# Decoding the first layer's weights one or two units earlier, with a clamp and a low part moved to GpSimd

## The chip, the cores and the metric

The kernel runs on one core of a Trainium2 chip. Its time is the device time of one execution in microseconds, and lower is better. TensorE (PE) does the matrix products, VectorE (DVE), ScalarE (ACT) and GpSimd (POOL) the elementwise work, and SyncE (SP) issues the transfers from and to HBM.

## What is computed

An attention over columns, followed by two feed-forward layers without biases. N is 6016 tokens, C is 256, the hidden width is 2048:

```python
qn = q / (norm(q, axis=1) + 1e-06)          # q, k, v: 6016 x 256
kn = k / (norm(k, axis=1) + 1e-06)
s = kn.T @ qn / tau                          # 256 x 256
a = exp(s - s.max(-1)); a /= a.sum(-1) + 1e-09
x = v @ a                                    # 6016 x 256
h = x @ w_in;  x = (h * cos(h)) @ w_out      # first layer
h = x @ w_in2; out = (h * sigmoid(h)) @ w_out2   # second layer
```

The weights lie in HBM as 64-bit floating-point numbers, and the kernel turns them into 32-bit ones itself.

## The kernel before

**Stages.** The scores are summed over the tokens while q and k arrive. Softmax follows at about 49 us. From there the first layer runs over blocks of 512 tokens, and later the second layer beside it. The stretch of this case is the first 135 us. v @ a is never formed: `a` is multiplied into w_in, in four pieces called folds (`fold`, L705, tile `pw`), and block after block of v is multiplied with the folded weights (`wa`).

**Units.** The loop over `units` (L1143 on) handles one block of 512 tokens and one pair of 128-column parts of the hidden width in each turn. The first 16 turns alternate between blocks 0 and 1 in pairs of turns, so that unit 0 and 1 are of block 0, unit 2 and 3 of block 1, unit 4 and 5 of block 0 again with the next fold's weights. In turn i the program issues: the 12 matmuls of the first product (`emit_h`, L792, tile `h`); the matmuls of one fold in turns 3, 6 and 10; the split of the last unit's result into a high and a low part (`emit_split`, ACT `hi` L798, DVE `lo` L799); the cosine (ACT L1138, tile `t`) and the product with it (DVE L1140); some steps of decoding; then the 12 matmuls of the second product of the unit two turns back (`emit_o1`, L812, tile `o`). Turns 0, 2, 4, 8 and 12 need a small bound first (`bound_piece`, matmuls L439, DVE L446 and L447, tile `bound` or `o` with `smalls`), from which the cosine's scale comes; it needs the largest entry of the new fold (DVE L457) and the range of each 128 tokens (`firsts`, DVE L427). Products `h` and folds `pw` use two rooms of PSUM in turn, so that a fold has to wait until the product of the unit before the last has left its room.

**Decoding.** Each matrix of the first layer comes in four pieces of 1024 numbers for each of 128 partitions: W1 (tile `w`, raw `raw_w`), one for each fold, and WO1 (tile `wv_wo`, raw `raw_wo`, result `wo`). A piece takes these steps, each a call with a name of two letters, the second of them W or O for the matrix:

- l: the load, a transfer on SP's queue (L279).
- b, begin: ACT takes the magnitude of the upper word (L345), POOL rounds the lower word (L299).
- c, clamp: DVE limits the magnitude (L304) and shifts it (L312).
- j, join: DVE puts the sign in (L318), POOL adds the lower word (L321).
- s, split (WO1 alone): ACT writes the high part (L364), POOL the low part (L365).

Fold k needs the join of W1's piece k. The other names in the tables below are: x0 and x1, the range of v's block 0 and 1 (`span_of_first`, L427); lv, the load of block 1 (L410, tile `vraw`, which has one buffer); s1 and v1, its high part on ACT (L486) and its low part on DVE (`low`, L489, tile `xlo`); v0, the low part of block 0 on POOL; rs, the inverse sums of softmax (L685, L686); f, e, l and w with a number, the matmuls of a fold, its high part (ACT L714), its low part (DVE L736) and its largest entries (L457).

**What sets the order.** Every engine works through its instructions in the order in which the program issues them. The order of the steps is written by hand, in the string `BEFORE` for what comes ahead of the first unit and in the table `EARLY` for the turns: 'amid' ahead of the split, 'mid' between cosine and product, 'outer' behind the product. An engine that waits holds back all that stands behind it.

Of the kernel before, what the change touches and what calls it, by code (L numbers as in the profile page):

```python
# [9 lines left out]
F32 = mybir.dt.float32  # L10
# [5 lines left out]
AF = mybir.ActivationFunctionType  # L16
ALU = mybir.AluOpType
# [5 lines left out]
CH = C // P  # L23
# [7 lines left out]
BLOCKS = [(sum(SIZES[:i]), n) for i, n in enumerate(SIZES)]  # L31
# [27 lines left out]
THEN = ['', '', 'jO s0', '']  # L59
SIDE = [7, 11, 15, 20]  # L60
JOINED = 22
BEFORE = 'v0 sO T0 T1 bW rs f00 x0 lv l00 f01 w00 l01 w01 tb x1 s1 l'
TURNS = 16
FORMING = {
    12: 'A0', 13: 'A1', 15: 'B0', 16: 'B1', 17: 'V', 18: 'V', 19: 'V A2', 20: 'A3', 21: 'B2', 22: 'B3'
}
DOUBLED = (17, 22)
EARLY = {
    'amid': {3: 'f1', 6: 'f2', 10: 'f3'},
    'mid': {0: 'v1'},  # L70
    'outer': {
# [3 lines left out]
    },  # L75
}
assert sum(GROUPS) == NCK
# [3 lines left out]
PASSES = ((0, 0), (1, 0), (0, 1))  # L81
# [146 lines left out]
def direct(ctx, tc, qk, vT, tau, w_in1, w_out1, w_in2, w_out2, outT, dp, kept, within):  # L228
    nc = tc.nc
# [35 lines left out]
    class Weights:  # L265
# [123 lines left out]
    def columns(t):  # L389
        return t.rearrange("p (h b) -> p b h", h=2)  # L390
# [127 lines left out]
    rs = pp.tile([P, CH], F32, name="rs")  # L518
    W1 = w_in(w_in1, "w1", to=w1, pool=pp, bufs=4, size=LARGE)
# [3 lines left out]
        parts=[[t[:, i].rearrange("p m (f e) -> p (m f) e", e=C) for i in range(2)] for t in wo1],  # L523
# [5 lines left out]
    raw_v, low_v = {}, {}  # L529
# [3 lines left out]
        "v0": lambda: low_v.pop(0)(nc.gpsimd),  # L533
        "x0": lambda: span_of_first(0, raw_v.pop(0)),
        "lv": lambda: raw_v.update({1: load_v(1)}),
        "x1": lambda: span_of_first(1, raw_v[1]),
        "s1": lambda: low_v.update({1: split_v(1, raw_v.pop(1))}),
        "v1": lambda: low_v.pop(1)(),
        "l": WO1.load,
        "lW": W1.load,  # L540
        "bW": W1.begin,
        "aW": lambda: W1.begin(low="act"),
        "cW": W1.clamp,
        "jW": W1.join,
        "bO": WO1.begin,
        "aO": lambda: WO1.begin(low="act"),
# [5 lines left out]
    def steps_of(names):  # L552
        for name in names.split():
            calls[name]()
# [201 lines left out]
    T = [sc.tile([P, NS, HB], F32, name=f"t{k}") for k in range(2)]  # L756
    HI, LO = [[sc.tile([P, NU, HB], F32R, name=f"{s}{k}") for k in range(2)] for s in ("hi", "lo")]
# [7 lines left out]
    def flat(t):  # L765
        return plain_part(t).rearrange("p (s n) -> p s n", s=2)
# [17 lines left out]
    def emit_h(u):  # L784
        b, m = u
        n = BLOCKS[b][1]
        x = xparts[1, b]
        hp = ready.pop() if ready else h_tile(f"h{b}_{m}")
        for s in range(2):
            todo = [(wa_at(i, a, 2 * m + s), columns(x[k][:, a, :n])) for i, k in PASSES for a in range(CH)]  # L790
            for i, (lhsT, rhs) in enumerate(todo):
                nc.tensor.matmul(hp[:, s, :n], lhsT, rhs, start=(i == 0), stop=(i == len(todo) - 1))  # L792
        return hp

    def emit_split(i, u):
        n = BLOCKS[u[0]][1]
        t, hi, lo = [flat(x[i % 2]) for x in (T, HI, LO)]
        nc.scalar.activation(hi[:, :, :n], t[:, :, :n], AF.Copy)  # L798
        nc.vector.tensor_tensor(out=lo[:, :, :n], in0=t[:, :, :n], in1=hi[:, :, :n].bitcast(F32), op=ALU.subtract)  # L799
        return hi, lo  # L800

    def o1_room(b):
        if (1, b) not in state:
# [330 lines left out]
    def cosine_in(i, h):  # L1134
        b, m = units[i]
        out = flat(T[i % 2])
        j = m // 2 * FIRST + b
        nc.scalar.activation(out, h, AF.Sin, bias=half_pi, scale=smalls[:, j : j + 1] if b < FIRST else small[b])  # L1138
        steps_of(EARLY["mid"].get(i, ""))
        nc.vector.tensor_tensor(out=out, in0=h, in1=out, op=ALU.mult)  # L1140

    units = [(i // 2 % 2, i // 4 * 2 + i % 2) for i in range(TURNS)] + [(FIRST, m) for m in range(NPAIR)]
    LAG = 2  # L1143
    parts = {}
    pend = None
    vs = []
    for i, u in enumerate(units):
        b, m = u
        if i == TURNS - 1:
            pro.close()  # L1150
            rp = ctx.enter_context(tc.tile_pool(name="rp", bufs=1))
            wf = [rp.tile([P, 2, 2, 4, P], F32R, name=f"wf{k}") for k in range(4)]
            Y = rp.tile([P, NU, HB], F32, tag="y", name="y")
            stage = rp.tile([P, 2, NS, P], F32R, name="stage")
            seeds = [rp.tile([P, HB], F32, name=s) for s in ("p7", "u2", "spare")]
            WI2 = w_in(w_in2, "wi2", forms=sink("wi2"))
            WO2 = w_out(w_out2, "wo2", forms=sink("wo2"))
        hp = emit_h(u)
        bounded = i in (4, 8, 12, TURNS - 1, TURNS + 6)
        if bounded:  # L1160
            emit_o1(units[i - LAG], parts[i - LAG], (0,))
        if i in (0, 2):
            bound_piece(0, (b,), o1_room(b)[:, 0])
        steps_of(EARLY["amid"].get(i, ""))
        if pend is not None:
            parts[pend] = emit_split(pend, units[pend])
        if i == TURNS + 6:
            bound(FIRST + 1, o1_room(FIRST + 1)[:, 0])
        elif bounded:
            ready.append(h_tile(f"bound{i}"))  # L1170
            if i < TURNS - 1:
                bound_piece(i // 4, range(FIRST), ready[0][:, 1])
            else:
                bound(FIRST, ready[0][:, 1])
        cosine_in(i, hp)
        pend = i
        steps_of(EARLY["outer"].get(i, ""))
        if i >= TURNS:
            for k, (ts, ds) in enumerate(zip((wa, wo1), kept)):
                if m % 2 == k:  # L1180
                    nc.sync.dma_start(out=ds[m // 2], in_=ts[m // 2].bitcast(F32))
# [24 lines left out]
        if i >= LAG:
            v = units[i - LAG]
            emit_o1(v, parts.pop(i - LAG), (1,) if bounded else (0, 1))
            if v[1] == NPAIR - 1:
                queue_x2(v[0])  # L1210
            if i >= TURNS:
                step()
            if i in DOUBLED:
                step()
# [175 lines left out]
    def first_layer(j, u, p, q, o):  # L1390
        k, k2 = (j - 1) % 2, j % 2
# [46 lines left out]
        if j < 2:  # L1438
            step()
        if j == 0:  # L1440
            parts[pend] = emit_split(pend, units[pend])
        while left and (j == 1 or len(left) > 2):
            emit_left()
        o_high()
# [194 lines left out]
```

## Time and profile before

| what | before |
|---|---|
| three runs, us | 1011.61, 1009.19, 1011.33 (median 1011.33) |
| the profiled execution, us | 1012.3 |
| its span from first to last instruction, us | 1010.4 |
| PE busy | 987.2 us, 98% of the span |
| DVE, ACT, POOL busy | 82%, 77%, 41% of the span |
| mean granted clock of TensorE | 0.993 of full speed |
| folds 1, 2 and 3 start at, us | 72.05, 96.02, 128.49 |

All times of the profile are in microseconds from the span's start, for that one execution. A granted clock of 1.00 is the higher of TensorE's two levels, 2.4 GHz; 0.50 is the lower one, 1.2 GHz. Busy PE isn't PE at its peak: at the lower level the same matmuls count as busy for longer.

### The profile page before, as it was taken

What the parts mean: (1) busy time and instruction counts of PE and PEld (TensorE: products, weight loads), DVE (VectorE), ACT (ScalarE), POOL (GpSimd) and SP (SyncE); (2) the same over time, 40 slices, a digit from 0 to 9 for tenths busy, and PEclk for the clock granted to TensorE, in tenths of its full rate; (3) what the DMA queues carried; (4) which work ended last, traced back from release to release, by engine and by line L of the source; (5) the groups of instructions that cost most, each with busy time, mean ns of one, the idle gap of its engine ahead of it and who ended that gap; (6) DMA issues with size and microseconds to landing.
All of it is one profiled execution on the core that took longest, in us unless ns stands there. A gap on an engine that the chain in (4) does not pass through costs nothing.

```text
span 1010.4 us, 18715 instructions
## 1 busy us (share of the span) xinstructions
PE 987.2 (98%) x7072; PEld 929.4 (92%) x7072; DVE 826.5 (82%) x1282; ACT 778.0 (77%) x1435; POOL 412.4 (41%) x386
## 2 busy tenths in 40 slices
PE   9988899999999999999999999999999999999998
PEld 8856778889999999999999999999999999999997
DVE  6795757987888787878874789999999999999972
ACT  6764546678988988888886888888888888887863
POOL 4443339837686787786564111111111111111100
PEclk9998989999999999999999999999999999999999
DMA  9931004734334344243369840220220121121101
GB/s 340 376 105 63 1 1 162 278 123 136 136 126 157 137 145 156 106 172 117 144 239 377 333 183 12 84 95 18 79 95 27 69 95 34 63 95 34 36 22 40
DMA packets 35012, 126.59 MB, mean 125 GB/s; under 512 B 3170, under 2 KB 4450, under 8 KB 30178
## 3 DMA queue, kind: packets, MB, share of 16 engines
q1 hardware_dynamic: 34770, 125.12, 33.6%
q8 instruction: 57, 0.93, 0.4%
q14 instruction: 41, 0.34, 0.1%
q10 hardware_dynamic: 144, 0.20, 0.1%
HBM read 73.01 MB, written 52.30 MB: 124 GB/s over the span
## 4 chain that ended last, share of the span: by engine, by line
PE 83%; DVE 8%; POOL 3%; issue 2%; DMA 2%; ACT 1%; SPq 0%; DVEq 0%; POOLq 0%; ACTq 0%
PE o L1026 20%; PE xz L1026 20%; PE o L1377 16%; PE ys L1026 15%; PE o L812 3%; DVE lo L799 2%; PE pw L705 2%; PE o L1066 2%; DMA qk<-qk_dram 2%; DVE t L1140 1%; PE S L582 1%; PE h L792 1%; POOL w1form L1000 1%; PE xz L1055 1%; PE ys L1055 1%
## 5 line engine op out<-in xcount | busy, mean ns | idle before, releaser
L842 DVE TENSOR_TENSOR lo<-t,hi 128x768 fp32r<-128x768 f32 (+1 forms) x176 | 194.7, 1116 | 29.2 <-ACT hi L834 29.1
L829 POOL TENSOR_TENSOR t<-t 128x256 f32<-128x256 f32 x88 | 64.6, 734 | 356.6 <-DVE t L826 312.8
L834 ACT ACTIVATE hi<-t 128x768 fp32r<-128x768 f32 (+1 forms) x176 | 168.8, 959 | 26.7 <-PE o L1026 25.8
L1377 PE MATMUL o<-hi,wo 128*128 128x512 f32 x512 | 142.0, 380 | 0.0
L1026 PE MATMUL o<-hi,wo 128*128 128x256 f32 x770 | 134.6, 275 | 0.0
L1026 PEld LDWEIGHTS o<-hi,wo 128*128 128x128 f32 x770 | 116.9, 192 | 0.0
L1026 PE MATMUL o<-lo,wo 128*128 128x256 f32 x385 | 105.9, 275 | 0.0
L1377 PEld LDWEIGHTS o<-hi,wo 128*128 128x128 f32 x512 | 87.4, 190 | 6.8
L1431 DVE TENSOR_TENSOR xz<-xz,t 128x512 f32<-128x512 f32 x64 | 44.7, 699 | 41.7 <-ACT t L1425 40.8
L1377 PE MATMUL o<-lo,wo 128*128 128x512 f32 x256 | 76.1, 380 | 0.0
L1026 PEld LDWEIGHTS ys<-xhi,wf 128*128 128x128 f32 x384 | 67.7, 190 | 7.6 <-ACT u L1467 0.5
L1026 PE MATMUL ys<-xhi,wf 128*128 128x256 f32 x384 | 74.3, 275 | 0.4 <-ACT u L1467 0.3
L1026 PEld LDWEIGHTS o<-lo,wo 128*128 128x128 f32 x385 | 73.9, 192 | 0.0
L1026 PE MATMUL xz<-xhi,wa 128*128 128x256 f32 x384 | 71.8, 276 | 0.0
L1535 ACT ACTIVATE ys<-xz 128x256 f32<-128x256 f32 x88 | 32.4, 368 | 45.8 <-PE xz L1026 44.8
L1026 PEld LDWEIGHTS xz<-xhi,wa 128*128 128x128 f32 x384 | 62.9, 191 | 3.3
L1026 PE MATMUL xz<-x2hi,wf 128*128 128x256 f32 x352 | 65.8, 275 | 0.0
L1026 PE MATMUL xz<-x2hi,wa 128*128 128x256 f32 x352 | 65.8, 275 | 0.0
L812 PE MATMUL o<-hi,wo 128*128 128x512 f32 (+1 forms) x256 | 64.0, 372 | 0.0
L821 DVE TENSOR_TENSOR t<-t 128x512 f32<-128x512 f32 x88 | 60.2, 685 | 0.1
L1565 ACT ACTIVATE t<-t 128x512 f32<-128x512 f32 x88 | 55.6, 632 | 2.2 <-DVE t L1076 2.1
L1026 PE MATMUL o<-hi,late 128*128 128x256 f32 x308 | 53.8, 275 | 0.0
(273 smaller groups left out, 3139.2 us busy)
## 6 DMA issues: line engine op xcount, KB each, us to landing
qk<-qk_dram SPq DMA_DIRECT2D x22, 512.0 KB, 7.6
x2hi<-xshi SPq DMA_DIRECT2D x11, 896.0 KB, 5.2
x2lo<-xslo SPq DMA_DIRECT2D x11, 896.0 KB, 7.3
wi_dram<-stage SPq DMA_DIRECT2D x8, 1024.0 KB, 3.8
wo_dram<-stage SPq DMA_DIRECT2D x8, 1024.0 KB, 4.3
vraw<-vT_dram SPq DMA_DIRECT2D x11, 512.0 KB, 4.0
outT_dram<-q SPq DMA_DIRECT2D x22, 256.0 KB, 2.0
xshi<-t SPq DMA_DIRECT2D x10, 512.0 KB, 5.3
```

The lines of the kernel that those rows point to most:

```text
L705: nc.tensor.matmul(pws[j, a], ET[:, d, a * P : (a + 1) * P], w1[:, d, j * TB : (j + 1) * TB], start=(d == 0), stop=(d == CH - 1),)
L799: nc.vector.tensor_tensor(out=lo[:, :, :n], in0=t[:, :, :n], in1=hi[:, :, :n].bitcast(F32), op=ALU.subtract)
L812: nc.tensor.matmul(o[:, e, :n], wo1_at(i, f)[:, e * P : (e + 1) * P], columns(parts[k][:, s, :n]), start=(f == 0 and (i, k) == PASSES[0]), ...
L821: eng.tensor_tensor(out=t[:, 4:6, :c], in0=t[:, 0:1, :c].to_broadcast([P, 2, c]), in1=t[:, 1:3, :c], op=ALU.subtract)
L829: eng.tensor_tensor(out=t[:, 7, :c], in0=t[:, 3, :c], in1=t[:, 6, :c], op=ALU.subtract)
L834: nc.scalar.activation(hi[:, sl, :c], t[:, 1:][:, sl, :c], AF.Copy)
L842: nc.vector.tensor_tensor(out=lo[:, sl, :c], in0=t[:, 1:][:, sl, :c], in1=hi[:, sl, :c].bitcast(F32), op=ALU.subtract)
L1026: nc.tensor.matmul(out, w(p, ka), columns(x[r][:, kb - 1]), start=(start and i == 0), stop=(stop and i == 2), skip_group_check=True,)
L1377: nc.tensor.matmul(o[:, e], wo1_at(i, f)[:, e * P : (e + 1) * P], columns(parts[k][:, s]), start=(f == 0 and (i, k) == PASSES[0]), stop=(f ...
L1431: nc.vector.tensor_tensor(out=xz[k], in0=xz[k], in1=sines[:, 1], op=ALU.mult)
L1535: nc.scalar.activation(y2, x2, AF.Copy)
L1565: nc.scalar.activation(t[:, 0:2], t[:, 0:2], AF.Silu)
```

## The change

- The clamp of W1's piece 1 moves from DVE to POOL (`kW`), ahead of the first unit, and the shift that followed it on DVE stands alone (`zW`, in turn 0).
- The low part of v's block 1 (v1) moves from DVE, ahead of unit 0's product, to POOL.
- x0 stands ahead of rs. x1 moves behind the bound of unit 0, to 'mid' of turn 0. The issue of WO1's next load ('l') moves from the end of `BEFORE` to turn 0, and s1 to the end of `BEFORE`.
- The joins of W1's pieces 1, 2 and 3 stand in turns 2, 4 and 8 (before: 1, 5 and 9), the clamps of pieces 2 and 3 in 'mid' of turns 4 and 8 (before: 'outer' of 5 and 8).
- The steps of WO1: begins in turns 1, 5 and 9 (before 1, 6 and 10), clamps in 2, 5 and 9 (before 2, 7 and 11), joins in 3, 7 and 11 (before 4, 7 and 11), the load of piece 3 in turn 4 (before 5), splits in a new place, 'inner', between the split of a unit and its cosine, of turns 4, 8 and 12 (before 'outer' of 5, 8 and 12).
- Unit 2's first product runs its eight matmuls with the high part of v ahead of the four with the low part; before, and in all other units, each half of the product has its six in one piece.
- In turn 2 the low part of unit 1 stands behind unit 2's product on DVE.

The lines of the changed kernel are one to seven further down in the decoding and fold functions, and 10 to 18 in the loop (L312 is L313, L365 is L370, L705 is L712, L799 is L817).

```diff
-BEFORE = 'v0 sO T0 T1 bW rs f00 x0 lv l00 f01 w00 l01 w01 tb x1 s1 l'
+BEFORE = 'v0 sO T0 T1 bW kW x0 rs f00 lv l00 f01 w00 l01 w01 tb s1'
...
 EARLY = {
-    'amid': {3: 'f1', 6: 'f2', 10: 'f3'},
-    'mid': {0: 'v1'},
+    'amid': {2: 'jW', 3: 'f1', 6: 'f2', 10: 'f3'},
+    'inner': {4: 'sO', 8: 'sO', 12: 'sO'},
+    'mid': {0: 'v1 x1', 4: 'cW', 8: 'cW'},
     'outer': {
-        0: 'cW', 1: 'bO jW', 2: 'cO lW', 3: 'e1 l10 l11 bW w10 w11', 4: 'jO', 5: 'cW jW sO l',
-        6: 'e2 l20 l21 bO w20 w21', 7: 'cO jO bW', 8: 'cW sO', 9: 'jW',
-        10: 'e3 l30 l31 bO w30 w31', 11: 'cO jO', 12: 'sO',
+        0: 'zW l', 1: 'bO', 2: 'cO lW', 3: 'e1 l10 l11 jO bW w10 w11', 4: 'jW l', 5: 'bO cO',
+        6: 'e2 l20 l21 w20 w21', 7: 'jO bW', 8: 'jW', 9: 'bO cO',
+        10: 'e3 l30 l31 w30 w31', 11: 'jO',
     },
 }
...
+        def shift(self):
+            self.clamped.append(self.begun.pop(0))
+            self.shift_word(self.clamped[-1][2])
...
-        "v1": lambda: low_v.pop(1)(),
+        "v1": lambda: low_v.pop(1)(nc.gpsimd),
...
+        "kW": lambda: W1.clamp_word(W1.begun[0][2], nc.gpsimd),
+        "zW": W1.shift,
...
+        sets = [(s, PASSES) for s in range(2)]
+        if u == (1, 0):
+            sets = [(s, ps) for ps in (PASSES[:2], PASSES[2:]) for s in range(2)]
...
         steps_of(EARLY["amid"].get(i, ""))
         if pend is not None:
-            parts[pend] = emit_split(pend, units[pend])
+            emit_high(pend)
+            if i != 2:
+                emit_low(pend)
+        steps_of(EARLY["inner"].get(i, ""))
...
         cosine_in(i, hp)
+        if i == 2:
+            emit_low(pend)
```

`emit_high` and `emit_low` are the two lines of the former `emit_split`, ACT's `hi` and DVE's `lo`.

DVE from the end of softmax to the product of unit 0. `rs` holds the sums of softmax, `vraw` v's block 0 and then block 1, `pw` and `wa` the first fold, `o` the room of the bound, `t` and `h` the cosine and the product of unit 0. Before:

```order
L685 TENSOR_SCALAR rs<-rs 128x2
L686 RECIPROCAL rs<-rs 128x2
L427 TENSOR_REDUCE firsts<-vraw_401 128x2x4
L736 SCALAR_TENSOR_TENSOR wa_89<-pw_466,rs,wa_89 128x2x256
L457 TENSOR_REDUCE largest<-wa_89 128x1
L736 SCALAR_TENSOR_TENSOR wa_89<-pw_474,rs,wa_89 128x2x256
L457 TENSOR_REDUCE largest<-wa_89 128x1
L427 TENSOR_REDUCE firsts<-vraw_471 128x2x4
L446 TENSOR_REDUCE o_0_511<-o_0_511 128x1
L447 TENSOR_SCALAR smalls<-o_0_511 128x1
L489 TENSOR_TENSOR xlo_484<-vraw_471,xhi_483 128x1024
L1140 TENSOR_TENSOR t_492<-h_0_498,t_492 128x1024
```

After:

```order
L432 TENSOR_REDUCE firsts<-vraw_401 128x2x4
L692 TENSOR_SCALAR rs<-rs 128x2
L693 RECIPROCAL rs<-rs 128x2
L743 SCALAR_TENSOR_TENSOR wa_89<-pw_468,rs,wa_89 128x2x256
L462 TENSOR_REDUCE largest<-wa_89 128x1
L743 SCALAR_TENSOR_TENSOR wa_89<-pw_475,rs,wa_89 128x2x256
L462 TENSOR_REDUCE largest<-wa_89 128x1
L451 TENSOR_REDUCE o_0_509<-o_0_509 128x1
L452 TENSOR_SCALAR smalls<-o_0_509 128x1
L432 TENSOR_REDUCE firsts<-vraw_472 128x2x4
L1158 TENSOR_TENSOR t_490<-h_0_496,t_490 128x1024
L313 TENSOR_SCALAR w_118<-w_118 128x2x512
```

The range of block 0 stands ahead of the inverse sums, the bound of unit 0 (L451, L452) ahead of the range of block 1, and neither the low part `xlo` nor, behind the product, a clamp of `w` is left on DVE.

POOL from the low part of v's block 0 on. `raw_w` and `w` are W1's pieces 1 and 2 by their numbers, `raw_wo` and `wv_wo` WO1's piece 1, `wo` its result. Before:

```order
L489 TENSOR_TENSOR xlo_438<-vraw_401,xhi_437 128x1024
L365 TENSOR_TENSOR wo_0_93<-wv_wo_405,wo_0_93 128x1024
L299 TENSOR_SCALAR raw_w_403<-raw_w_403 128x1024
L299 TENSOR_SCALAR raw_wo_408<-raw_wo_408 128x1024
L321 TENSOR_TENSOR w_118<-w_118,raw_w_403 128x2x512
L299 TENSOR_SCALAR raw_w_410<-raw_w_410 128x1024
L321 TENSOR_TENSOR wv_wo_538<-wv_wo_538,raw_wo_408 128x1024
L321 TENSOR_TENSOR w_118<-w_118,raw_w_410 128x2x512
L365 TENSOR_TENSOR wo_1_94<-wv_wo_538,wo_1_94 128x1024
```

After:

```order
L494 TENSOR_TENSOR xlo_438<-vraw_401,xhi_437 128x1024
L370 TENSOR_TENSOR wo_0_93<-wv_wo_405,wo_0_93 128x1024
L300 TENSOR_SCALAR raw_w_403<-raw_w_403 128x1024
L305 TENSOR_SCALAR w_118<-w_118 128x2x512
L494 TENSOR_TENSOR xlo_484<-vraw_472,xhi_483 128x1024
L300 TENSOR_SCALAR raw_wo_408<-raw_wo_408 128x1024
L322 TENSOR_TENSOR w_118<-w_118,raw_w_403 128x2x512
L322 TENSOR_TENSOR wv_wo_538<-wv_wo_538,raw_wo_408 128x1024
L300 TENSOR_SCALAR raw_w_410<-raw_w_410 128x1024
L370 TENSOR_TENSOR wo_1_94<-wv_wo_538,wo_1_94 128x1024
L322 TENSOR_TENSOR w_118<-w_118,raw_w_410 128x2x512
```

Two operations, the clamp of `w` and the low part of block 1, now stand ahead of the rounding of `raw_wo` and the first add of `w`; the low part of WO1's piece 1 now stands ahead of the second add of `w`, behind which it stood.

DVE in turns 4 to 6, from the bound of turn 4 to the product ahead of fold 2. `lo`, `hi` and `t` are those of the units, `w` is W1's piece 2. Before:

```order
L446 TENSOR_REDUCE bound_644<-bound_644 128x2
L447 TENSOR_SCALAR smalls<-bound_644 128x2
L1140 TENSOR_TENSOR t_492<-h_2_623,t_492 128x1024
L318 SCALAR_TENSOR_TENSOR wv_wo_538<-raw_wo_408,wv_wo_538 128x1024
L799 TENSOR_TENSOR lo_496<-t_492,hi_494 128x1024
L1140 TENSOR_TENSOR t_493<-bound_644,t_493 128x1024
L304 TENSOR_SCALAR w_118<-w_118 128x2x512
L312 TENSOR_SCALAR w_118<-w_118 128x2x512
L318 SCALAR_TENSOR_TENSOR w_118<-raw_w_410,w_118 128x2x512
L799 TENSOR_TENSOR lo_497<-t_493,hi_495 128x1024
L1140 TENSOR_TENSOR t_492<-h_2_695,t_492 128x1024
```

After:

```order
L451 TENSOR_REDUCE bound_648<-bound_648 128x2
L452 TENSOR_SCALAR smalls<-bound_648 128x2
L305 TENSOR_SCALAR w_118<-w_118 128x2x512
L313 TENSOR_SCALAR w_118<-w_118 128x2x512
L1158 TENSOR_TENSOR t_490<-h_2_625,t_490 128x1024
L319 SCALAR_TENSOR_TENSOR w_118<-raw_w_410,w_118 128x2x512
L817 TENSOR_TENSOR lo_494<-t_490,hi_492 128x1024
L1158 TENSOR_TENSOR t_491<-bound_648,t_491 128x1024
```

The clamp and the shift of `w` (L305, L313) moved ahead of a product, and the sign step of `w` (L319) one unit ahead, with `lo` and a product that stood between gone from in front of them; WO1's sign step left this stretch for the turn before. On SP's queue the transfers keep their order.

## Rows read from the trace of the kernel before

**Rows 1.** Waits of PE over the span: line, awaited; total us, times, longest us.

```profile
PE pw L705 <- POOL w L321: 9.7, 2, 5.1
PE pw L705 <- DVE t L1140: 1.7, 1, 1.7
...
PE o L812 <- DVE lo L799: 0.8, 1, 0.8
PE ys L1026 <- ACT u L1467: 0.3, 1, 0.3
```

**Rows 2.** PE's timeline: start us, us, engine, line, operation, [idle before, releaser].

```profile
62.24 1.10 PE L792 MATMUL h<-xhi,wa 128*128 128x512 f32 x4 [1.15 <-DVE t L1140]
...
72.05 3.67 PE L705 MATMUL pw<-w,ET 128*128 128x512 f32 x8 [1.65 <-DVE t L1140]
75.15 1.43 PE L812 MATMUL o<-hi,wo 128*128 128x512 f32 x4
...
96.02 6.47 PE L705 MATMUL pw<-w,ET 128*128 128x512 f32 x8 [4.61 <-POOL w L321]
101.92 1.43 PE L812 MATMUL o<-hi,wo 128*128 128x512 f32 x4
...
128.49 5.60 PE L705 MATMUL pw<-w,ET 128*128 128x512 f32 x8 [5.13 <-POOL w L321]
133.52 1.43 PE L812 MATMUL o<-hi,wo 128*128 128x512 f32 x4
```

**Rows 3.** Windows: sum, PE, PEld, DVE, ACT, POOL busy (x); clock, DMA share, GB/s.

```profile
70.00:72.00 2.00, 0.40 (x2) 0.00 (x0) 2.00 (x3) 0.01 (x1) 1.73 (x1) 1.00 0.54 125
...
96.00:98.00 2.00, 1.98 (x3) 0.95 (x4) 0.00 (x0) 0.00 (x0) 2.00 (x1) 0.50 0.04 14
102.00:104.00 2.00, 2.00 (x10) 1.57 (x9) 0.18 (x1) 1.48 (x3) 0.00 (x0) 1.00 0.00 0
```

**Rows 4.** DVE's timeline, from softmax to fold 2.

```profile
51.45 1.28 DVE L685 TENSOR_SCALAR rs<-rs 128x2 f32<-128x2 f32 x1
...
52.85 1.20 DVE L427 TENSOR_REDUCE firsts<-vraw 128x8 bf16<-128x1024 f32 x1
...
59.44 1.52 DVE L489 TENSOR_TENSOR xlo<-vraw,xhi 128x1024 fp32r<-128x1024 f32 x1
60.86 1.23 DVE L1140 TENSOR_TENSOR t<-h,t 128x1024 f32<-128x1024 f32 x1
...
67.31 3.46 DVE L799 TENSOR_TENSOR lo<-t,hi 128x1024 fp32r<-128x1024 f32 x1
...
77.06 1.41 DVE L736 SCALAR_TENSOR_TENSOR wa<-pw,rs,wa 128x512 fp32r<-128x512 f32 x2 [1.56 <-ACT wa L714]
...
90.63 0.69 DVE L312 TENSOR_SCALAR w<-w 128x1024 int32<-128x1024 int32 x1
91.36 1.23 DVE L318 SCALAR_TENSOR_TENSOR w<-raw_w,w 128x1024 int32<-128x1024 int32 x1
92.50 1.22 DVE L799 TENSOR_TENSOR lo<-t,hi 128x1024 fp32r<-128x1024 f32 x1
```

**Rows 5.** POOL's timeline in the same stretch.

```profile
50.28 2.42 POOL L489 TENSOR_TENSOR xlo<-vraw,xhi 128x1024 fp32r<-128x1024 f32 x1
52.66 2.38 POOL L365 TENSOR_TENSOR wo<-wv_wo,wo 128x1024 fp32r<-128x1024 f32 x1
55.12 1.28 POOL L299 TENSOR_SCALAR raw_w<-raw_w 128x1024 int32<-128x1024 uint32 x1
...
67.27 2.41 POOL L321 TENSOR_TENSOR w<-w,raw_w 128x1024 int32<-128x1024 int32 x1 [9.22 <-DVE o L446]
...
92.73 3.23 POOL L321 TENSOR_TENSOR w<-w,raw_w 128x1024 int32<-128x1024 int32 x1 [2.69 <-DVE w L318]
```

**Rows 6.** POOL's groups by form: the clamp of later pieces; busy us, mean ns, idle.

```profile
L304 POOL TENSOR_SCALAR wv_wi<-wv_wi 128x512 f32<-128x512 f32 x8 | 15.3, 1918 | 0.6
```

**Rows 7.** SP's timeline: the issue of the load of v's block 1.

```profile
54.12 0.37 SPq L410 DMA_DIRECT2D vraw<-vT_dram  x1
```

More of the change, by code (lines that the diff above doesn't have):

```diff
@@ L535, in direct @@
         "lv": lambda: raw_v.update({1: load_v(1)}),
-        "x1": lambda: span_of_first(1, raw_v[1]),
-        "s1": lambda: low_v.update({1: split_v(1, raw_v.pop(1))}),
-        "v1": lambda: low_v.pop(1)(),
+        "x1": lambda: span_of_first(1, raw_v.pop(1)),
+        "s1": lambda: low_v.update({1: split_v(1, raw_v[1])}),
+        "v1": lambda: low_v.pop(1)(nc.gpsimd),
         "l": WO1.load,
@@ L788, in emit_h, with emit_high, emit_low @@
         hp = ready.pop() if ready else h_tile(f"h{b}_{m}")
[L789 to L792, printed above, removed]
-        return hp
-    def emit_split(i, u):
-        n = BLOCKS[u[0]][1]
+        sets = [(s, PASSES) for s in range(2)]
+        if u == (1, 0):
+            sets = [(s, ps) for ps in (PASSES[:2], PASSES[2:]) for s in range(2)]
+        for s, ps in sets:
+            for i, k in ps:
+                for a in range(CH):
+                    nc.tensor.matmul(
+                        hp[:, s, :n],
+                        wa_at(i, a, 2 * m + s),
+                        columns(x[k][:, a, :n]),
+                        start=((i, k) == PASSES[0] and a == 0),
+                        stop=((i, k) == PASSES[-1] and a == CH - 1),
+                    )
+        return hp
+    def emit_high(i):
+        t, hi = [flat(x[i % 2]) for x in (T, HI)]
+        nc.scalar.activation(hi, t, AF.Copy)
+    def emit_low(i):
         t, hi, lo = [flat(x[i % 2]) for x in (T, HI, LO)]
-        nc.scalar.activation(hi[:, :, :n], t[:, :, :n], AF.Copy)
-        nc.vector.tensor_tensor(out=lo[:, :, :n], in0=t[:, :, :n], in1=hi[:, :, :n].bitcast(F32), op=ALU.subtract)
-        return hi, lo
+        nc.vector.tensor_tensor(out=lo, in0=t, in1=hi.bitcast(F32), op=ALU.subtract)
+        parts[i] = hi, lo
     def o1_room(b):
@@ L1440, in first_layer @@
         if j == 0:
-            parts[pend] = emit_split(pend, units[pend])
+            emit_high(pend)
+            emit_low(pend)
         while left and (j == 1 or len(left) > 2):
```

## The prediction

> **What bounds the kernel now.** I read the waits of PE first, because PE is busy for 98% of the span and only its idle time and its slow time can be won. Two folds wait 9.7 us for POOL's add of the weights, one fold 1.7 us for a product of DVE, and one second product 0.8 us for a low part; the next entry behind these that lies after the stretch is 0.3 us [rows 1]. The timeline gives their places: 1.15 us ahead of unit 2's first product, 1.65 ahead of fold 1, 4.61 ahead of fold 2, 5.13 ahead of fold 3 [rows 2].
>
> The second price is the clock. The eight matmuls of fold 1 last from 72.05 to 75.15, 3.10 us; those of fold 2 from 96.02 to 101.92, 5.90 us, and of fold 3 from 128.49 to 133.52, 5.03 us [rows 2]. The window from 96 us on shows a granted clock of 0.50, which is 1.2 GHz, and that from 102 us on 1.00 again, while the idle 1.65 us ahead of fold 1 left it at 1.00 [rows 3]. So the two long waits cost another 2.80 and 1.93 us. Waits and clock together: 1.15 + 1.65 + 4.61 + 5.13 + 2.80 + 1.93 = 17.3 us lie in this stretch.
>
> Third, why the adds are late. DVE and POOL get in each other's way. The low part of unit 1 starts at 67.31 and takes 3.46 us, the same operation at 92.50 takes 1.22; it ends at 70.77, 1.09 us after the end of POOL's add at 69.68 [rows 4, 5]. The other way round, POOL's add for fold 2 takes 3.23 us instead of 2.41, behind that 1.22 us low part [rows 4, 5]. Even the sums `rs`, two numbers for each partition, take 1.28 us and end with POOL's operation [rows 4, 5]. The range `firsts` (1.20 us under POOL's 52.66 to 55.04) and the products, which read PSUM, show no such stretch [rows 4, 5]. I therefore let clamp, shift, sign step, low part and `rs` on DVE take turns with everything on POOL, and nothing else.
>
> The Trainium skill has the same on its page SBUF — State Buffer, section "Who interferes with whom": one pair of ports is shared and locked for a whole instruction. From that its page Perfetto Trace Analysis, section "Optimizing Scalar/DVE Operations", draws a rule against this change: handing work from one of the two engines to the other might not help. By the rows, the work that goes to POOL here gets dearer, and I count that below; what gains is the order.
>
> **The start.** Block 1 of v has one buffer, and its load is issued at 54.12, right after `firsts` of block 0 (52.85 + 1.20 = 54.05) [rows 4, 7]. `firsts` now takes the place of `rs` and ends at 51.45 + 1.20 = 52.65; POOL's low part of block 0 reads the buffer until 52.70 [rows 5], so the load comes 1.35 us sooner. That the next load isn't issued with it any more costs and brings nothing: the order on SP's queue stays, nothing makes the second wait for the first, and the work on POOL below covers it. `rs` asks at 52.65, just before POOL gives way at 52.70, and so ends where it did. Ahead of unit 0's product the low part goes (59.44, 1.52 us); bounds are 0 and 1.5 us, I take 0.7, since the cosine still waits for the bound of fold 0, which stays. Unit 2's first product then starts at 61.5 instead of 62.24. Eight matmuls with the high part (2.59/12 us each, as unit 2's run from 62.24 to 64.83) reach to 63.2.
>
> POOL: the rounding ends at 56.40 [rows 5]. The clamp has no row for 1024 numbers there; its nearest is 1.918 us for 512 [rows 6], so 3.84; the lower bound is the rounding's 1.28 us for 1024 [rows 5], the upper one 5. End at 60.24, low part of v1 plus 2.42: 62.66, ahead of 63.2, so the two passes hide it. DVE's shift (0.69) waits for that: 63.35. POOL's rounding (1.28) and DVE's low part of unit 0 (1.22) take turns: 65.85. Product of unit 1, 1.23: 67.1. The bound's two small operations (between nothing and the 1.28 of `rs`; I take 0.4): 67.5. Sign step 1.23: 68.7. Add 2.41: 71.1. Each handing over overlaps by a tenth, so **fold 1 at 71.0** [rows 4, 5]. The product of unit 2, which ended the wait before, now stands ahead of the low part of unit 1 and ends at 69.9. Gain 1.05.
>
> **Fold 2.** PE has 96.02 - 4.61 - 72.05 = 19.36 us of work from fold 1's start [rows 2]: 90.4 at best. Fold 1's low parts on DVE come 77.06 - 72.05 = 5.0 us behind it and take 1.41 [rows 2, 4]: 77.4. Then WO1's sign step, 1.23, and POOL's add, 2.41: 81.1. Now the pair of ports is asked for by the low part of unit 3 (1.22), the rounding (1.28), the clamp (0.7, like the shift), WO1's low part (2.38) and the shift (0.69), 6.3 us: 87.4. Product 1.23, sign step 1.23, a low part that gets ahead of the add as it did at 92.50, 1.22, and the add, 2.41 [rows 4, 5]: 93.4; less the overlaps, **93.0**. The bound of turn 4 stands behind that low part (81.1 + 1.22 + 0.4 = 82.7), which is some 0.8 us later than PE would ask for its result; so PE is ready at 91.2 and waits 1.8 instead of 4.61. That is next to the 1.65 that left the clock alone [rows 3], so fold 2 takes 3.10 and ends at 96.1 instead of 101.92. Gain so far 5.8.
>
> **Fold 3.** PE's work is 3.10 + (128.49 - 5.13 - 101.92 = 21.44) [rows 2]: 117.5. The steps stand as for fold 2, but WO1's sign step in turn 7 has no low parts of a fold ahead of it. Bounds of the wait are 0 and fold 2's 1.8; I take 0.8: **118.3**, end 121.4 instead of 133.52. WO1's steps on ACT in turns 4 and 8 stand ahead of the cosine; they wait for POOL's add (81.1) and are covered by the bound, which is there at 82.7. The end is PE's, with no wait of any size behind [rows 1], so all of it stays.
>
> Sum: 1.05 + (4.61 - 1.8 - 0.8) + 2.80 + (5.13 - 0.8) + 1.93 = 12.1. The span goes from 1010.4 to 998.3, the execution from 1012.3 to 1000.2; the median of the runs lies 1.0 under the profiled one, so **999.2**.
>
> **The rivals.**
> - `rs` comes too late for the gap at 52.70 and waits for WO1's low part until 55.04 [rows 5]. Fold 0 is then 2.3 us later, and with little cover up to fold 1 all is 2.2 later: 1001.4. For it: 0.05 us of lead, where it had 1.2. Against: it asks first. Chance 0.20.
> - The clock falls at fold 2 all the same, as 1.8 us is above the 1.65 that is proved; I charge 2.4, less than the 2.80 of a longer wait: 1001.6. Chance 0.10.
> - The clamp on POOL is as fast as the rounding, 1.28. Then the low part of v1 is done at 60.1, and fold 1 starts when PE is ready: (72.05 - 1.65 - 62.24) = 8.16 behind 61.5, at 69.7 [rows 2], 1.3 sooner: 997.9. Against it stands the 1.918 for half the numbers [rows 6]. Chance 0.05. The Trainium skill's GPSIMD Engine Reference, section "4.1 Engine selection", calls one-input work there roughly line-rate; that bears on this case, and rows 6 disagree.
> - The change doesn't do what it says: the adds move, but their waits for the pair of ports grow by as much, and only fold 1's 1.05 stays: 1010.3. Chance 0.04.
> - Slower: WO1's split on ACT, now ahead of the cosine in turns 4, 8 and 12, holds it up until POOL's add is through. If that is later than the room of PSUM that PE needs next, each of the three turns stops PE for an add (3.23 [rows 5]) and the clock (2.80, from fold 2): 3 x 6.03 = 18.1, more than the 12.1 that is won: 999.2 + 18.1 = 1017.3. It decides from the point where the add ends about one turn of PE (5.2 us) behind the split of the unit; by my sum the add ends at 81.1, and the cosine of that turn can't start before the bound at 82.7 anyway. Chance 0.03.
>
> **How the numbers follow.** The forecast has 0.58. Downwards the range takes the fast clamp (1.3), no wait at fold 3 (0.8) and the 0.8 of the late low part [rows 1], which may go as WO1's last piece is decoded sooner: 996.5. Upwards it takes either of the first two rivals and most of both: 1003.5. Left out are the last two, and the ends of the others. A measurement here tells about 0.3%, 3 us, from no change: 1010.3 counts as the same, 1017.3 as slower, so 0.93 faster, 0.04 same, 0.03 slower.
>
> **What would show it.** Right: `rs` ends by 52.8; POOL's clamp takes 3.8 us; fold 1 starts near 71.0, fold 2 near 93 with a wait under 2.5 us and all eight matmuls in 3.1 us, fold 3 near 118; the waits of PE on POOL's add fall from 9.7 to about 3 to 4 us. Wrong: a granted clock of 0.50 in the window of fold 2, an `rs` of more than 2 us, or a new wait of PE for products in turns 4 and 8 that takes back what the folds won.

## The result and the profile after

The changed kernel takes 1000.5 us (median of 6 runs, 999.54 to 1001.8), before 1011.35 (median of 6). The ratio is 0.9896, 95% interval 0.9884 to 0.9909: faster by 10.5 us, 9.2 to 11.7, by the ratio. Forecast were 999.2 and a range of 996.5 to 1003.5.

The profiled execution took 999.54 us, its span 997.8, which is 12.6 less than before. But 1.0 of these is not the change's: softmax was through sooner, as the first copy into `ET` shows (DVE, start us, us; before, then after).

```profile
50.26 0.42 DVE L675 COPY ET<-pt 128x256 f32<-128x256 f32 x1 [0.32 <-PE pt L674]
```

```profile
49.25 0.42 DVE L682 COPY ET<-pt 128x256 f32<-128x256 f32 x1 [0.32 <-PE pt L681]
```

Everything up to that copy is the same in both kernels, and it starts between 49.2 and 51.4 us in the profiles below. Most of that is the arrival of q and k, for which PE waits 0.8 us in the profile after, 1.5 in the one before and 2.8 in the latest. So I compare by **the stretch**: from the start of this copy to the first matmul behind fold 3 (`o`). Before it is 133.52 - 50.26 = 83.26 us, with the end from [rows 2]. PE's timeline after:

```profile
60.47 1.97 PE L802 MATMUL h<-xhi,wa 128*128 128x512 f32 x8 [0.41 <-DVE t L1158]
...
70.01 3.70 PE L712 MATMUL pw<-w,ET 128*128 128x512 f32 x8 [0.81 <-POOL w L322]
73.15 1.43 PE L830 MATMUL o<-hi,wo 128*128 128x512 f32 x4
81.81 1.13 PE L802 MATMUL bound<-xhi,wa 128*128 128x512 f32 x4 [0.18 <-DVE smalls L452]
...
87.36 1.10 PE L802 MATMUL h<-xhi,wa 128*128 128x512 f32 x4
...
91.97 3.70 PE L712 MATMUL pw<-w,ET 128*128 128x512 f32 x8 [1.77 <-POOL w L322]
95.10 1.43 PE L830 MATMUL o<-hi,wo 128*128 128x512 f32 x4
...
117.90 3.70 PE L712 MATMUL pw<-w,ET 128*128 128x512 f32 x8 [1.36 <-POOL w L322]
121.03 1.43 PE L830 MATMUL o<-hi,wo 128*128 128x512 f32 x4
```

The stretch is 121.03 - 49.25 = 71.78 us, 11.48 shorter. All three folds wait for POOL's add, for 0.81, 1.77 and 1.36 us (before 1.65 for a product, then 4.61 and 5.13 for the add [rows 2]), and each runs its eight matmuls in 3.13 to 3.14 us. Before, folds 2 and 3 took 5.90 and 5.03 us for theirs, so 10.93 - 6.26 = 4.67 of the 11.48 us are the clock, and the rest is idle time that went. Behind the stretch the two profiles take the same, 1010.4 - 133.52 = 876.9 and 997.8 - 121.03 = 876.8 us. The waits of PE over the span (total, times, longest) and the window of fold 2 (last numbers: clock, DMA share, GB/s), which had 0.50 before [rows 3]:

```profile
PE pw L712 <- POOL w L322: 3.9, 3, 1.8
...
PE o L830 <- DVE lo L817: 1.2, 2, 0.8
```

```profile
92.00:94.00 2.00, 2.00 (x5) 1.02 (x6) 1.97 (x3) 1.02 (x1) 1.52 (x1) 1.00 0.00 0
```

The start, on DVE and then on POOL:

```profile
50.43 1.21 DVE L432 TENSOR_REDUCE firsts<-vraw 128x8 bf16<-128x1024 f32 x1
51.56 0.16 DVE L692 TENSOR_SCALAR rs<-rs 128x2 f32<-128x2 f32 x1
...
60.24 1.78 DVE L313 TENSOR_SCALAR w<-w 128x1024 int32<-128x1024 int32 x1
61.94 2.62 DVE L817 TENSOR_TENSOR lo<-t,hi 128x1024 fp32r<-128x1024 f32 x1
...
70.97 0.68 DVE L305 TENSOR_SCALAR wv_wo<-wv_wo 128x1024 f32<-128x1024 f32 x1
```

```profile
51.64 2.38 POOL L370 TENSOR_TENSOR wo<-wv_wo,wo 128x1024 fp32r<-128x1024 f32 x1
...
55.46 3.62 POOL L305 TENSOR_SCALAR w<-w 128x1024 f32<-128x1024 f32 x1
59.04 2.42 POOL L494 TENSOR_TENSOR xlo<-vraw,xhi 128x1024 fp32r<-128x1024 f32 x1
61.55 1.97 POOL L300 TENSOR_SCALAR raw_wo<-raw_wo 128x1024 int32<-128x1024 uint32 x1
```

`rs` got in between the two operations of POOL and took 0.16 us. POOL's clamp takes 3.62 us for what DVE does in 0.68. DVE's shift and low part (0.69 and 1.22 by themselves, [rows 4]) take 1.78 and 2.62 while POOL works. Where I say below that an operation waits for the ports, I mean this: it is recorded longer than by itself while the other of the two engines works.

The chain of fold 2's add, on DVE and then on POOL, and below the dots, from fold 3's chain, the sign step that came out longer than summed (DVE) and what it waited for (POOL):

```profile
81.68 1.60 DVE L305 TENSOR_SCALAR w<-w 128x1024 f32<-128x1024 f32 x1
83.31 2.78 DVE L313 TENSOR_SCALAR w<-w 128x1024 int32<-128x1024 int32 x1
86.00 1.21 DVE L1158 TENSOR_TENSOR t<-h,t 128x1024 f32<-128x1024 f32 x1
87.14 1.38 DVE L319 SCALAR_TENSOR_TENSOR w<-raw_w,w 128x1024 int32<-128x1024 int32 x1
...
111.89 2.55 DVE L319 SCALAR_TENSOR_TENSOR w<-raw_w,w 128x1024 int32<-128x1024 int32 x1
```

```profile
80.48 2.25 POOL L300 TENSOR_SCALAR raw_w<-raw_w 128x1024 int32<-128x1024 uint32 x1
82.81 2.73 POOL L370 TENSOR_TENSOR wo<-wv_wo,wo 128x1024 fp32r<-128x1024 f32 x1
88.66 3.25 POOL L322 TENSOR_TENSOR w<-w,raw_w 128x1024 int32<-128x1024 int32 x1 [3.12 <-DVE w L319]
...
110.38 2.75 POOL L370 TENSOR_TENSOR wo<-wv_wo,wo 128x1024 fp32r<-128x1024 f32 x1
```

### The profile page after: what moved, and what is told of

Read it like the earlier page. It is cut to its first block, busy times and chain, and to the rows that moved or that the text cites. A ratio compares the mean times of both kernels' runs of the same rounds, so it can differ in the third digit from the quotient of the medians.

```text
span 997.8 us, 18717 instructions
## 1 busy us (share of the span) xinstructions
PE 983.0 (99%) x7072; PEld 927.4 (93%) x7072; DVE 830.5 (83%) x1280; ACT 777.5 (78%) x1435; POOL 418.3 (42%) x388
## 4 chain that ended last, share of the span: by engine, by line
PE 89%; DVE 6%; issue 2%; POOL 1%; ACT 1%; DMA 1%; SPq 0%; ACTq 0%; POOLq 0%
PE o L1044 20%; PE xz L1044 20%; PE o L1400 17%; PE ys L1044 15%; PE o L830 4%; PE S L589 3%; PE h L802 2%; PE o L1084 2%; DVE lo L817 1%; PE pw L712 1%; DVE t L1158 1%; POOL w L322 1%; PE xz L1073 1%; PE ys L1073 1%; PE xz L1355 1%
```

## Experiments

Each edit is against the changed kernel. Each stretch is from one profile. In the six profiles with the changed start in full, fold 1 begins 20.68 to 20.80 us behind the copy, while the runs' times of one kernel move by 1 us and more; so a verdict on a small effect rests on the stretch, and differences of 0.1 us are at its limit. Ratios are to the kernel before.

**The start alone.** The table of the turns from 3 on as before:

```diff
-    'inner': {4: 'sO', 8: 'sO', 12: 'sO'},
-    'mid': {0: 'v1 x1', 4: 'cW', 8: 'cW'},
+    'mid': {0: 'v1 x1'},
...
+        3: 'e1 l10 l11 bW w10 w11', 4: 'jO', 5: 'cW jW sO l',
+        6: 'e2 l20 l21 bO w20 w21', 7: 'cO jO bW', 8: 'cW sO', 9: 'jW',
+        10: 'e3 l30 l31 bO w30 w31', 11: 'cO jO', 12: 'sO',
```

> The changed kernel with the steps of turns 3 to 12 where they were before; the start (clamp and low part on POOL, the range ahead of the sums, the join in turn 2, unit 1's low part behind unit 2's product) stays changed. Measure: the stretch from the start of the first copy into ET to the end of fold 3's matmuls, 83.26 us before (50.26 to 133.52) and 71.78 after (49.25 to 121.03). My theory: the start is worth only what fold 1 gained, 1.05 us, and the two long waits come back with the low clock: stretch 82.2 (81.5 to 83.5), folds 2 and 3 each with a wait over 4 us and a window at clock 0.50, time about 1010. Rival: the start, by taking POOL's and DVE's turns out of each other's way, carries the later folds too: stretch under 78, time under 1006.

1010.2 us (ratio 0.9986, 0.9976 to 0.9995). PE's timeline:

```profile
94.72 6.06 PE L712 MATMUL pw<-w,ET 128*128 128x512 f32 x8 [4.58 <-POOL w L322]
100.21 1.43 PE L830 MATMUL o<-hi,wo 128*128 128x512 f32 x4
126.77 5.39 PE L712 MATMUL pw<-w,ET 128*128 128x512 f32 x8 [5.12 <-POOL w L322]
131.60 1.43 PE L830 MATMUL o<-hi,wo 128*128 128x512 f32 x4
```

The stretch is 131.60 - 49.69 = 81.91, 1.35 us shorter than before. Fold 1 starts 0.99 sooner, much as in the changed kernel; 0.61 of the 1.35 are the two slow folds, which took 10.32 instead of 10.93 us. Both long waits are back as they were, and so are the slow folds (5.49 and 4.83 us).

**The turns alone.** Start, split of unit 1 and pass order as before, with the steps of turns 3 to 12 as changed.

> The opposite: the start and turns 0 to 2 as before, the steps of turns 3 to 12 as changed. My theory: stretch 71.78 + 1.05 = 72.8 (72 to 74), fold 1 with its wait of about 1.65 for a product, folds 2 and 3 with waits under 2.5 us at the full clock, time about 1001.5. Rival: the start carries the gain: stretch over 78, time over 1006.

1000.76 us (0.9897, 0.9879 to 0.9914), stretch 121.99 - 49.24 = 72.75. PE's timeline:

```profile
92.94 3.70 PE L712 MATMUL pw<-w,ET 128*128 128x512 f32 x8 [1.80 <-POOL w L322]
...
118.86 3.70 PE L712 MATMUL pw<-w,ET 128*128 128x512 f32 x8 [1.34 <-POOL w L322]
```

Folds 2 and 3 wait 1.80 and 1.34 us at the full clock, fold 1 waits 1.65 for a product again. So the turns carry 83.26 - 72.75 = 10.5 us and the start the rest, 0.97. The rival falls with both runs. Which of the moves in the turns carry the 10.5 us, those of W1's joins or those of WO1's steps, no run took apart.

**A longer wait.** POOL's low part of WO1's piece 1 is written a second time:

```diff
-    'inner': {4: 'sO', 8: 'sO', 12: 'sO'},
+    'inner': {4: 'dO', 8: 'sO', 12: 'sO'},
...
+        def split_twice(self):
+            i, v = self.joined[0]
+            hi, lo = self.parts[i]
+            self.split()
+            nc.gpsimd.tensor_tensor(out=lo, in0=v, in1=hi.bitcast(F32), op=ALU.subtract)
```

> The changed kernel with POOL's low part of WO1's piece 1 done twice (the same result is written again), which puts about 2.4 us more ahead of fold 2's add. It prices a longer wait by itself. My theory: fold 2 waits about 4.2 instead of 1.77 us, the clock falls as it did at 4.61 and 5.13 us, and the fold's eight matmuls take about 5.9 instead of 3.1 us: stretch 71.78 + 2.4 + 2.8 = 77.0, time about 1005.7. Rival: the low clock before came from something else than the wait (the length of the slow stretch as a whole, or the work ahead of it): only 2.4 is added, stretch 74.2, time about 1002.9.

1002.51 us (0.9909, 0.9891 to 0.9926), stretch 124.93 - 50.30 = 74.63. PE's timeline, and a window of that fold:

```profile
94.18 5.37 PE L719 MATMUL pw<-w,ET 128*128 128x512 f32 x8 [2.97 <-POOL w L322]
98.98 1.43 PE L837 MATMUL o<-hi,wo 128*128 128x512 f32 x4
```

```profile
94.00:96.00 2.00, 1.82 (x2) 0.83 (x3) 1.97 (x2) 1.25 (x2) 1.56 (x2) 0.54 0.00 0
```

The time was that of the rival, its reason was not: the clock did fall, and the fold took 98.98 - 94.18 = 4.80 us instead of 3.13. What I had wrong was the wait: it grew by 1.2, not by 2.4 us. DVE's shift slipped in between POOL's two low parts, and only the sign step waited for the second (2.58 us instead of 1.38). On DVE, then on POOL:

```profile
84.31 2.79 DVE L313 TENSOR_SCALAR w<-w 128x1024 int32<-128x1024 int32 x1
...
88.16 2.58 DVE L319 SCALAR_TENSOR_TENSOR w<-raw_w,w 128x1024 int32<-128x1024 int32 x1
```

```profile
83.81 2.74 POOL L370 TENSOR_TENSOR wo<-wv_wo,wo 128x1024 fp32r<-128x1024 f32 x1
86.63 2.74 POOL L376 TENSOR_TENSOR wo<-wv_wo,wo 128x1024 fp32r<-128x1024 f32 x1
```

So 1.2 us of wait and 1.67 of clock make up the 2.85 by which the stretch is longer. The wait alone was changed here, and the clock fell with it.

**The splits later.** WO1's splits behind the adds of W1:

```diff
-    'inner': {4: 'sO', 8: 'sO', 12: 'sO'},
...
-        ... 4: 'jW l', 5: 'bO cO', ... 8: 'jW', 9: 'bO cO', ... 11: 'jO',
+        ... 4: 'jW l', 5: 'sO bO cO', ... 8: 'jW', 9: 'sO bO cO', ... 11: 'jO', 12: 'sO',
```

> The changed kernel with WO1's splits back behind the adds of W1 (ahead of the other steps of turns 5 and 9, and in turn 12 as before), so that POOL's low part of 2.4 to 2.7 us stands behind the add that a fold waits for. My theory: that low part is in the chain of the add (the shift on DVE took 2.78 us under it), so folds 2 and 3 lose most of their waits of 1.77 and 1.36; against that the second product of the unit behind the fold may wait up to 1.2 us for the low part. Stretch 69 to 70.5, time 998 to 999.5. Rival: the chain is held by the rounding and the pair of low part and add just as well, and nothing changes (71.5 to 72.1), or the second products lose what the folds win.

999.32 us (0.9886, 0.9867 to 0.9905), stretch 118.98 - 49.43 = 69.55. Fold 2 waits for nothing and fold 3 for 0.32. So POOL's low part was in the chain of the add. A part of it is paid back one unit later, on PE; the second of these waits lies behind the end of the stretch, so the stretch leaves it out:

```profile
96.97 1.13 PE L802 MATMUL h<-xhi,wa 128*128 128x512 f32 x4 [0.55 <-DVE t L1158]
...
122.71 1.13 PE L802 MATMUL h<-xhi,wa 128*128 128x512 f32 x4 [0.58 <-DVE t L1158]
```

because WO1's shift (2.77) and a unit's low part (2.43) now wait for POOL's on DVE:

```profile
90.67 2.77 DVE L313 TENSOR_SCALAR wv_wo<-wv_wo 128x1024 int32<-128x1024 int32 x1
93.36 2.43 DVE L817 TENSOR_TENSOR lo<-t,hi 128x1024 fp32r<-128x1024 f32 x1
95.71 1.21 DVE L1158 TENSOR_TENSOR t<-h,t 128x1024 f32<-128x1024 f32 x1
```

**WO1's clamps later too.** The same with `cO` from turns 5 and 9 to the end of 6 and 10:

> WO1's splits behind the adds, as in the run with the later splits, and WO1's clamps and shifts moved one turn further, from 5 and 9 to 6 and 10. In that run the shift (2.77) and a low part (2.43) waited for POOL's low part and pushed the product behind them, for which PE waited 0.55 and 0.58 us. My theory: without clamp and shift there the low part of the unit takes its turn first and the two waits go: stretch 69.0 to 69.6 against 69.55, and 1.1 us less in all: time 998 to 998.7. Rival: the low part of the unit waits for POOL's in any case, the product is as late, and nothing is won; or WO1's add, now later, holds something behind the fold: 999.3 or more.

996.87 us (0.9863, 0.9847 to 0.9880), stretch 118.09 - 49.33 = 68.76. Both waits of 0.55 and 0.58 are gone; the folds wait 0.79, 0.20 and 0.27. The waits that went are those expected; stretch and time both came out below the expected range, and what won the rest isn't shown.

**The clamp on DVE.** The clamp of W1's piece 1 back from POOL:

```diff
-BEFORE = 'v0 sO T0 T1 bW kW x0 rs f00 lv l00 f01 w00 l01 w01 tb s1'
+BEFORE = 'v0 sO T0 T1 bW x0 rs f00 lv l00 f01 w00 l01 w01 tb s1'
...
-        0: 'zW l', 1: 'bO',
+        0: 'cW l', 1: 'bO',
```

> The changed kernel with the clamp of W1's piece 1 back on DVE, in turn 0 ahead of the shift; the rest, the low part of v1 on POOL too, stays. It prices what the clamp's place brings or costs. My theory: POOL's clamp (3.62 us there, 0.68 on DVE) stands in the way: without it POOL's low part of v1 starts when its high part is there (57.7 instead of 59.04), and DVE has 0.7 more; fold 1 loses most of its wait of 0.81, stretch (first copy into ET to the end of fold 3's matmuls) 70.9 to 71.3 against 71.78, time 999.7 to 1000. Rival: the clamp on DVE asks for the ports while POOL writes the low part, pays a whole operation for it (about 2.4) and comes out later than with POOL: stretch over 72.2.

999.81 us (0.9892, 0.9876 to 0.9909), stretch 120.54 - 49.88 = 70.66, 1.12 shorter, a little more than my theory gave; the rival falls. Fold 1 starts 69.56 - 49.88 = 19.68 us behind the copy, against 20.76. On DVE, with POOL's low part of v1 now at 57.92 to 60.34:

```profile
60.87 1.42 DVE L305 TENSOR_SCALAR w<-w 128x1024 f32<-128x1024 f32 x1
62.32 0.69 DVE L313 TENSOR_SCALAR w<-w 128x1024 int32<-128x1024 int32 x1
62.92 1.22 DVE L817 TENSOR_TENSOR lo<-t,hi 128x1024 fp32r<-128x1024 f32 x1
```

Clamp and shift together end at 63.01, 13.1 us behind the copy into `ET`. In the changed kernel the shift alone ends at 62.02, 12.8 behind it, and then the low part waits for POOL's rounding and ends at 64.56 (15.3 behind); here it ends at 64.14 (14.3 behind). So the move of the clamp costs 1.1 us, and what the start gains comes from its other parts.

**The low part of unit 1 in its place,** ahead of unit 2's product.

```diff
             emit_high(pend)
-            if i != 2:
-                emit_low(pend)
+            emit_low(pend)
...
-        if i == 2:
-            emit_low(pend)
```

> The changed kernel with the low part of unit 1 back ahead of unit 2's product on DVE. Before, that low part lost the ports to POOL's add and the product behind it set fold 1. My theory: the low part gets in ahead of the add now, as the sign step ends right before it, and pushes the add by its 1.2 us: fold 1 1.0 us later, stretch 72.8, time about 1001.5. Rival A: it loses the ports as before, and the product comes 2.3 us later: stretch 74.1. Rival B: the add is as early, the product has slack, nothing changes: 71.8.

1001.07 us (0.9903, 0.9886 to 0.9919), stretch 123.10 - 50.51 = 72.59, 0.81 longer. The low part gets in ahead of the add, which then takes 3.23 instead of 2.40 us, and fold 1 waits 1.64: as expected, and neither rival.

**The range behind the sums,** one run (1000.65 us):

```diff
-BEFORE = '... kW x0 rs f00 lv ...'
+BEFORE = '... kW rs f00 x0 lv ...'
```

> The changed kernel with the range of v's block 0 behind the inverse sums and fold 0's first half again, as before; the load of block 1 then comes about 1.2 us later. My theory: the load's lead is worth little, since POOL's clamp lasts until 59.1 in any case; PE is ready for fold 1 1.1 us later and the wait of 0.81 there takes most of it: stretch 71.8 to 72.4 against 71.78, POOL's add for fold 1 at the same distance from ET. Rival: the load is what the start gains from: the stretch grows by the whole 1.2, to 73.0.

The stretch is 122.06 - 50.28 = 71.78, the same to the hundredth. The load of block 1 is issued 1.4 us later and it costs nothing, as POOL's clamp holds up the low part of that block until 9.9 us behind the copy here and 9.8 in the changed kernel. With the clamp on DVE, where the low part starts 8.0 us behind the copy, the lead was not tested.

**Unit 2's product in one pass,** one run (1000.54 us). Its two lines are taken out.

> The changed kernel with unit 2's first product in the usual order, so that its first two matmuls with v1's low part come after four, not after eight. My theory: POOL's low part ends at 61.46, PE would ask for it at 61.35, so at most some 0.2 us is waited, and the wait of 0.81 at fold 1 takes it: stretch 71.7 to 71.9. Rival: the pass order is needed for PE to go on: stretch over 72.3.

The stretch is 121.88 - 49.92 = 71.96, and PE starts the low part's matmuls in that product at 62.24, right behind the end of POOL's low part (62.19). Most of the 0.18 by which the stretch is longer is fold 3's wait, 1.47 instead of 1.36; fold 1 starts 20.81 behind the copy, against 20.76. The pass order brings nothing that I can measure.

**W1's clamps behind the product,** in the same turns 4 and 8, one run (1003.78 us):

```diff
-    'mid': {0: 'v1 x1', 4: 'cW', 8: 'cW'},
+    'mid': {0: 'v1 x1'},
...
-        ... 4: 'jW l', ... 8: 'jW', ...
+        ... 4: 'cW jW l', ... 8: 'cW jW', ...
```

> The changed kernel with the clamps and shifts of W1's pieces 2 and 3 behind the product of units 4 and 8 again, in the same turns (before, they stood behind those of units 5 and 9). It asks what of the gain is the turn and what the place ahead of the product. My theory: the turn is what counts; clamp and shift wait for POOL's rounding and low part in either place, and the product goes ahead in the meantime: stretch 71.0 to 72.5 against 71.78. Rival: the place ahead of the product is needed, as clamp and shift behind it add their own 1.4 us and a wait of up to 2.7 to each of two folds: stretch over 73.5.

The stretch is 125.13 - 51.36 = 73.77: the rival's number, at one fold instead of two. PE:

```profile
93.54 3.70 PE L712 MATMUL pw<-w,ET 128*128 128x512 f32 x8 [1.59 <-POOL w L322]
96.68 1.43 PE L830 MATMUL o<-hi,wo 128*128 128x512 f32 x4
120.29 5.40 PE L712 MATMUL pw<-w,ET 128*128 128x512 f32 x8 [2.18 <-POOL w L322]
125.13 1.43 PE L830 MATMUL o<-hi,wo 128*128 128x512 f32 x4
```

At fold 2 the place ahead of the product even costs: fold 2 starts 93.54 - 51.36 = 42.18 us behind the copy here and 42.72 in the changed kernel, where the product stands behind clamp and shift. For fold 3 it is the other way round: the product of unit 8 comes late,

```profile
112.06 1.23 DVE L1158 TENSOR_TENSOR t<-h,t 128x1024 f32<-128x1024 f32 x1 [2.71 <-ACT t L1156]
113.20 1.39 DVE L305 TENSOR_SCALAR w<-w 128x1024 f32<-128x1024 f32 x1
```

as ACT's split of WO1, now ahead of the cosine, waits for POOL's add (it starts at 109.86, the add ends at 109.82); before, DVE waited 1.36 us for that cosine, here 2.71. Behind the product, clamp and shift wait for all of it; ahead of it, they use that time. And fold 3, with 2.18 us of wait, falls to the low clock (0.60 and 0.54 granted in the two windows from 120 to 124 us): 4.84 us instead of 3.13, which is 1.71 of the 1.99 us by which the stretch is longer.

**The two that gained, together:** WO1's splits and clamps later, and the clamp of W1's piece 1 on DVE.

> The later splits and clamps of WO1 together with the clamp of W1's piece 1 back on DVE: the two that made the changed kernel faster by themselves (stretch 68.76 and 70.66 against 71.78). My theory: they lie at different folds and add up: fold 1's wait 0.3 instead of 0.8, the low part of unit 0 without its wait, folds 2 and 3 at 0.2 to 0.3; stretch 67.6 to 68.2, time 995.8 to 996.5. Rival: fold 1's lead is eaten by fold 2's chain, which follows the units and not the start: stretch 68.5 to 68.9, time as that of the later splits and clamps, 996.9.

996.57 us (0.9848, 0.9835 to 0.9862), stretch 118.26 - 50.33 = 67.93. The folds wait 0.42, 0.20 and 0.37 us. By the stretch it gains 0.83 on the run with the later splits and clamps; by the times, 996.57 and 996.87, the two can't be told apart. Both beat the changed kernel by more than 3 us.

## Why the prediction was right

Measured from the copy into `ET`, point by point:

- **Fold 1** was to start 1.05 us sooner; it did by 21.79 - 20.76 = 1.03. The chain came as summed: DVE's shift ended 12.77 us behind the copy (13.09 by the sum), the product of unit 1 at 16.45 (16.84), the add at 20.71 (20.84). The sum held that the clamp gets dearer on POOL and that the order gains, and so it was: the low part of unit 1 behind the product is worth 0.81, and POOL's clamp costs 1.1 of what could be had. The other gains of the start, v1's low part on POOL and the new place of x1, no run moved alone; that they carry the rest is argued and not shown. My sum showed POOL's chain as the last to come, and I didn't set beside it the chain with the clamp left on DVE, which is shorter.
- **Fold 2** was to start 3.0 sooner and to end 5.8 sooner; it was 3.04 and 5.81. Wait 1.77 (1.8 forecast), clock 1.00. The chain of the add was right down to its turns on the ports: counted from fold 1's start, DVE's shift ended at 16.08 us (16.4 by the sum) and the add at 21.90 (22.0). PE was ready 91.97 - 1.77 - 70.01 = 20.19 us behind fold 1, 0.83 later than its 19.36 us of work, and 0.8 was summed. But the bound is only a part of this: it delays PE by 0.37, with 0.18 named as a wait, and another 0.37 came ahead of the product at 87.36, right behind the end of DVE's late product (86.00 + 1.21). That second half was not in the sum, so the agreement of this term is in part luck.
- **Fold 3** is the term that was mis-sized: wait 1.36 instead of 0.8, which is nearly all of the difference between 11.48 and 12.1. I had taken a value between nothing and fold 2's. The sign step of piece 3 took 2.55 us, where my chain for fold 2 has 1.23: it waited for POOL's low part of WO1 (110.38 to 113.13), and with that part behind the add, in the run with the later splits, the wait fell to 0.32.
- **The clock** stayed, but with less room than the chance of 0.10 says: 1.80 us of wait left it (turns alone), 2.18 did not (clamps behind the product).
- **Time and range.** The runs gave 1000.5 and not 999.2; 0.6 of these 1.3 us is fold 3, the rest lies within the spread of one kernel's runs (999.54 to 1001.8). By its own three terms the lower end of the range is 999.2 - 2.9 = 996.3 and not 996.5, which changes nothing. The prediction names [rows 4, 5] for products that take no longer under POOL's work, but no product in these rows runs under an operation of POOL; the trace has one, at 70.69, which takes 1.21 us under POOL's rounding (69.77 to 71.74).
- **The rivals.** `firsts` ended 0.05 us ahead of the end of POOL's operation (51.64 and 51.69), and `rs` got through. The waits did not move elsewhere, but for the small ones shown. The fast clamp on POOL didn't happen: it took 3.62 us, against 0.68 on DVE. The Trainium skill's GPSIMD Engine Reference, section "4.1 Engine selection", calls one-input work there roughly line-rate; for this clamp the trace does not agree. The slower rival, ACT's split ahead of the cosine, is a real mechanism: it is seen at unit 8 in the run with the clamps behind the product. In the changed kernel DVE's clamp and shift fill the time.
- The rule against the change, that work handed from DVE to POOL might not help (the Trainium skill, Perfetto Trace Analysis, "Optimizing Scalar/DVE Operations"), is borne out for the clamp, which costs 1.1 us of the stretch on POOL; for v1's low part no run tested it.

The runs' gain, 10.5 us with an interval of 9.2 to 11.7, agrees with the stretch's 11.48.

## What to carry to other kernels

Where two engines take turns on a port, count every operation of both as one queue, and look for the one that needn't stand ahead of the result that is waited for: moving a 2.4 us low part behind the add was worth 2.2 us of the stretch, where moving the clamp to the other engine cost 1.1. A wait of the matrix engine is priced with the slow work behind it: here the eight matmuls behind 2.18 us of wait took 1.7 us longer than those behind 1.80. Measure a local change from a point that both kernels share; here the arrival of data moved the whole span by a microsecond or two.

## What I had not expected

- An engine that waits for the ports gets them between two queued operations of the other: the shift between POOL's two low parts took 2.79 us, not 5.5, and the wait grew by 1.2 instead of 2.4.
- The clock: fold waits of 1.36, 1.77 and 1.80 us left the granted clock alone, 2.18 and 2.97 were followed by eight matmuls of 4.84 and 4.80 us, and 4.58 and 5.12 by 5.49 and 4.83, where 3.13 is the time at the full clock. The price of a fall isn't in step with the length of the wait.
- A clamp with two constants takes 3.62 us on POOL for 1024 numbers, the rounding, also of one input and two constants, 1.10 with DVE idle (in the kernel before, at 98.41) and 1.27 to 1.37 at the start, where DVE reduces and reads PSUM.
